# Emptying two kinds of PSUM accumulators on ScalarE or on VectorE, as a planner chooses

## The chip, the core and the metric

The kernel runs on one core of one Trainium2 chip. The metric is device time in microseconds (us); lower is better. TensorE multiplies matrices into PSUM; ScalarE and VectorE can read PSUM, GpSimd cannot. Each engine takes its instructions in the order in which they stand in its own queue, and engines wait for one another through semaphores. In the views of the profile PE is TensorE, PEld its loading of weights, ACT ScalarE, DVE VectorE, POOL GpSimd, and SP the engine that issues nearly all DMAs; L763 is line 763 of the kernel.

## The reference

For 8 batches and 8 heads (sequence 576, head size 64) the attention keeps only the scores that lie within tau of their row's maximum. Its result goes through a gate made by a causal convolution over the sequence, and through two 512x512 products:

```python
scores = scale * np.matmul(q, k.transpose(0, 1, 3, 2))
thresh = np.max(scores, axis=-1, keepdims=True) - tau
scores = np.where(scores >= thresh, scores, -1000000000.0)
attn = np.exp(scores - np.max(scores, axis=-1, keepdims=True))
attn = attn / (np.sum(attn, axis=-1, keepdims=True) + 1e-09)
x = np.matmul(attn, v)          # then heads side by side: [batch, 576, 512]
...
gate_pre += conv_w[k][None, None, :] * xp[:, k:k + S, :]      # k = 0..4, x shifted
gate = 1.0 / (1.0 + np.exp(-gate_pre))
val = x @ w_val
return (gate * val @ w_out).astype(np.float32)
```

Here `scale` is 1/8, tau is 0.02, and all arrays are float32.

## The kernel before, in words

**The work.** A *job* is one batch and one pair of heads (32 jobs); a batch is four jobs. A job has nine *tiles* of scores, each 128 queries by 576 keys: eight for one head, and one that takes the last 64 queries of both heads. Products of full precision are made from parts: a high part (`kh`, `xh`, `gh`) in a fast format and the rest (`kl`, `xl`, `gl`).

The steps of a tile, with their lines:

- TensorE computes the scores into a PSUM room `s` (L556): four matmuls of 288 columns, six for the tile of both heads.
- VectorE takes the negative row maximum, `nm` (L562).
- ScalarE computes `e`, the exponentials (L568), and the threshold from `nm` (L570).
- VectorE keeps the values over the threshold and sums them, `pp` (L589). Only after this is the room `s` free again. There are two such rooms, `s_90` and `s_91`, used in turn for nearly all of the run.
- GpSimd adds a small number to the sums (L609), VectorE takes reciprocals (L611), and GpSimd or ScalarE multiplies (L622, L618).
- TensorE transposes `pp` into a room `tp` (L678, in threes; two rooms), and ScalarE copies that to SBUF as `T` (L689).

When the tiles of half a job are done, TensorE multiplies `T` by the values `v` into an accumulator `acc` (L752). In batches 1 to 7 ScalarE copies this to `xT` (L763), in two pieces per job, of 320 and of 256 columns. In batch 0 VectorE does it, with a multiplication. From `xT` come the parts `xh` (ScalarE, L837) and `xl` (GpSimd, L321), and the convolution: its first tap on GpSimd (L847), four taps on VectorE (L854), in batch 0 on TensorE (L807), then the gate on ScalarE (L862).

After a batch's four jobs come its *products*: `x` by `w_val` into `acc`, gated by VectorE into `g` (L952), split into `gh` and `gl`, and `g` by `w_out` into `acc`. Here `wvh` and `woh` are the high parts of the weights, `wvl` and `wol` the rest; twelve matmuls (L924) make one accumulator of 320 or of 256 columns. ScalarE halves the outputs into `o` (L995), and SP sends them to memory. There are two accumulators, `acc_318` and `acc_319`. They serve the attended values and both products alike, and each is free again when it has been emptied.

**What sets the order.** No loop does. Every operation is first recorded as an `Op` with an engine, a due time, an estimated cost, an estimated time until others may use its result, what it comes after, and the rooms that it takes and gives back. Then `carry_out` (L153) plays the program through: again and again it looks for the operation that can begin earliest by the estimates, the one with the smaller due time among equals, and emits it there and then. The emitted order is fixed; on the chip each engine follows it and waits where its semaphores say. An operation may have several ways, each with its engine and cost; it then stands in the list of every such engine, and whichever can begin it earliest gets it. Before the change only the multiplications by reciprocals have two ways (GpSimd, ScalarE). TensorE gets what can begin, so products fill the time in which the next scores or transposes cannot. A table, `SHIFT`, moves due times by function, engine and phase of the run.

Of the kernel before, what the change touches and what calls it, by code (L numbers as in the profile page):

```python
# [16 lines left out]
ALU = mybir.AluOpType  # L17
# [9 lines left out]
LATE = 1  # L27
# [22 lines left out]
def tile_thresholded_attention_gated_mix(  # L50
# [14 lines left out]
    nc = tc.nc  # L65
# [127 lines left out]
    r_acc = Rooms(None, 0, None, None, None)  # L193
# [23 lines left out]
    r_xT = Rooms(mix, 2, [P, PAD + S], F32, "xT")  # L217
# [487 lines left out]
    class Half:  # L705
# [35 lines left out]
        def attended(self, k):  # L741
            t, j = self.t, self.j
            w, x0 = W[j], PAD + HALVES[j].start

            def attend():
                acc = self.acc = r_acc.take()
                T = self.T[:, :, 0:w]
                for c in (NKC, *range(NKC)):
                    for h, hs in enumerate(HEADS):
                        c0 = (2 * c + h) * D  # L750
                        chunk = 2 * NKC if c == NKC else h * NKC + c
                        nc.tensor.matmul(  # L752
                            acc[hs, :w], t.v[:, c0 : c0 + D], T[:, chunk, :],
                            start=c == NKC, stop=c == NKC - 1, skip_group_check=True,
                        )

            def evacuate():
                if j == 0:
                    t.xT = r_xT.take()
                if t.b < LATE:  # L760
                    nc.vector.tensor_mul(t.xT[:, x0 : x0 + w], self.acc[:, :w], self.R[:, W[0] - w :])
                else:
                    nc.scalar.copy(t.xT[:, x0 : x0 + w], self.acc[:, :w])  # L763

            cost = 5 * w / 600 + 0.1
            gives = [(r_T, lambda: self.T)]
            if j == 1:
                gives.append((r_v, lambda: t.v))
            made = op("PE", k - (1, 1.5)[j], cost, cost + 0.2, attend, [t.got_v, *self.copies], [r_acc], gives)
            cost = 0.31 if j == 0 else 0.255  # L770
            after = [made] if j == 0 else [made, t.got_x]
            gives = [(r_acc, lambda: self.acc)]
            if t.b < LATE:
                cost += 0.085
                after.append(self.inverses(k))
                gives.append((r_R, lambda: self.R))
            t.got_x = op("DVE" if t.b < LATE else "ACT", k - (3, 3.5)[j], cost, cost + 0.2, evacuate, after,
                         [r_xT] if j == 0 else [], gives)
            t.got_half.append(t.got_x)


# [124 lines left out]
    def products(batch, k, last):  # L906
        b = batch.b
        gs, g, o = {}, {}, {}
        taken = {}
# [77 lines left out]
        for f in range(NE):  # L987
            for j in range(2):
                def evacuate(m, f=f, j=j):
                    hs = HALVES[j]  # L990

                    def run():
                        if j == 0:
                            o[f] = r_o.take()
                        nc.scalar.mul(o[f][:, hs], taken["wo", f, j][:, 0 : hs.stop - hs.start], 0.5)  # L995

                    cost = 0.32 if j == 0 else 0.265
                    return op("ACT", k - 5, cost, cost + 0.2, run,
                              [m] + ([outs[f]] if j else []), [r_o] if j == 0 else [],
                              [(r_acc, lambda: taken["wo", f, j])])  # L1000

                outs[f] = product("wo", f, j, lambda c, i: gs[c][i], parts_of, evacuate)
                firsts.setdefault(f, outs[f])
# [117 lines left out]
```

## Time and profile before

| | |
|---|---|
| median of three runs | 733.68 us (733.28 to 734.31) |
| the profiled execution | 734.48 us, of which the program's span 732.6 us |
| TensorE busy | 721.2 us (98%), granted clock 1.0 throughout |
| ScalarE, VectorE, GpSimd busy | 621.4, 600.3 and 530.1 us |
| copies L763 and L995 | 56 and 64, all on ScalarE |

How to read it: "busy" is the union of an engine's instructions. A row of a view with `xcount` is a group of instructions; two numbers behind the bar are busy us and mean ns of one, and behind the next bar the idle time just before them with what ended it. "who <- by" in the view of waits names the engine that sat idle and the instruction that ended the wait. In a timeline, a row has the start, the length, the engine, the line and the operation.

### The profile page before, as it was taken

The numbers are of one execution on the slowest core, as the hardware profiler recorded it, in microseconds if no ns is written. First come the engines' busy times: TensorE is split into PE (matmuls) and PEld (weight loads), VectorE is DVE, ScalarE is ACT, GpSimd is POOL, SyncE is SP. The second block draws the span as 40 slices with busy tenths as digits, with TensorE's granted clock in tenths as the row PEclk, the third lists the DMA queues.
The fourth block names the chain that finished last, engine by engine and source line by source line (L and its number), as shares of the span: only waits on it lengthen the run. The fifth ranks groups of instructions, "written<-read, shape, count | busy, mean of one in ns | idle before, by whom it ended". The sixth has DMA issues, their size and how long they took to land.

```text
span 732.6 us, 16311 instructions
## 1 busy us (share of the span) xinstructions
PE 721.2 (98%) x5454; PEld 613.9 (84%) x5454; DVE 600.3 (82%) x1291; ACT 621.4 (85%) x1448; POOL 530.1 (72%) x886
## 2 busy tenths in 40 slices
PE   8989999999999999999999999999999999999998
PEld 4767778888898888888888888888888988888898
DVE  6899979999888888788888888888888888888730
ACT  6698889999899988888989889898989988888832
POOL 4876568778889757697778786897658887766331
PEclk9999999999999999999999999999999999999999
DMA  7755665636564655346655546555635465540001
GB/s 211 186 154 149 161 156 138 153 97 154 156 176 125 155 134 138 108 125 181 152 138 140 129 120 162 142 129 137 172 101 144 122 159 152 127 112 21 33 34 65
DMA packets 51588, 97.97 MB, mean 134 GB/s; under 512 B 9008, under 2 KB 9520, under 8 KB 51504
## 3 DMA queue, kind: packets, MB, share of 16 engines
q1 hardware_dynamic: 51264, 96.61, 51.1%
q8 instruction: 44, 0.72, 0.5%
q10 hardware_dynamic: 240, 0.31, 0.2%
q14 instruction: 40, 0.33, 0.1%
HBM read 34.62 MB, written 9.44 MB: 60 GB/s over the span
## 4 chain that ended last, share of the span: by engine, by line
PE 89%; ACT 4%; DVE 3%; DMA 2%; POOL 1%; issue 1%; SPq 0%; ACTq 0%; POOLq 0%
PE acc L924 26%; PE s L556 22%; PE acc L752 21%; PE tp L678 18%; ACT e L568 1%; PE acc L807 1%; DVE pp L589 1%; DVE nm L562 1%; DMA q_r<-qT 1%; ACT T L689 1%; DMA pre<-kT 0%; ACT pp L618 0%; ACT nm L570 0%; ACT xh L837 0%; DMA Q<-ql 0%
## 5 line engine op out<-in xcount | busy, mean ns | idle before, releaser
L562 DVE TENSOR_REDUCE nm<-s 128x1 f32<-128x576 f32 x288 | 214.1, 754 | 44.6 <-PE s L556 41.5
L589 DVE SCALAR_TENSOR_TENSOR pp<-s,nm,e 128x576 f32<-128x576 f32 x256 | 207.2, 813 | 33.2 <-ACT nm L570 29.2
L568 ACT ACTIVATE e<-s,nm 128x576 f32<-128x576 f32 x288 | 215.5, 748 | 19.8 <-DVE nm L562 14.8
L689 ACT COPY T<-tp 128x384 f32<-128x384 f32 x384 | 176.2, 487 | 26.2 <-PE tp L678 24.7
L678 PE MATMUL tp<-ident,pp 128*128 128x128 f32 x1152 | 175.3, 273 | 1.1 <-ACT T L689 1.1
L752 PE MATMUL acc<-T,v 128*64 128x256 f32 (+1 forms) x1280 | 169.3, 411 | 0.0
L622 POOL TENSOR_SCALAR pp<-pp,sums 128x576 f32<-128x576 f32 x165 | 137.6, 840 | 39.4 <-DVE sums L611 33.0
L556 PE MATMUL s<-KH,Q 128*128 128x288 f32 x496 | 152.2, 323 | 3.3 <-DVE pp L589 3.1
L678 PEld LDWEIGHTS tp<-ident,pp 128*128 128x128 f32 x1152 | 138.7, 140 | 7.2 <-ACT T L689 1.8
L556 PE MATMUL s<-KL,Q 128*128 128x288 f32 x496 | 138.2, 295 | 0.0
L752 PEld LDWEIGHTS acc<-T,v 128*64 128x64 f32 x1280 | 86.2, 136 | 61.5 <-issue 8.9
L556 PEld LDWEIGHTS s<-KH,Q 128*128 128x128 f32 x496 | 93.4, 188 | 29.0 <-issue 13.7
L854 DVE SCALAR_TENSOR_TENSOR pre<-xT,cw,pre 128x576 f32<-128x576 f32 x112 | 103.3, 922 | 9.1 <-POOL pre L847 8.9
L556 PEld LDWEIGHTS s<-KL,Q 128*128 128x128 f32 x496 | 93.6, 189 | 0.3
L570 ACT ACTIVATE nm<-nm,less 128x1 f32<-128x1 f32 x288 | 85.3, 296 | 0.0
L924 PE MATMUL acc<-gh,woh 128*128 128x320 f32 (+1 forms) x256 | 79.0, 309 | 0.0
L924 PE MATMUL acc<-xl,wvh 128*128 128x320 f32 (+1 forms) x256 | 78.5, 307 | 0.0
L924 PE MATMUL acc<-xh,wvl 128*128 128x320 f32 (+1 forms) x256 | 78.3, 306 | 0.0
L924 PE MATMUL acc<-xh,wvh 128*128 128x320 f32 (+1 forms) x256 | 78.0, 305 | 0.0
L924 PE MATMUL acc<-gl,woh 128*128 128x320 f32 (+1 forms) x256 | 77.9, 304 | 0.0
L924 PE MATMUL acc<-gh,wol 128*128 128x320 f32 (+1 forms) x256 | 77.5, 303 | 0.0
L609 POOL TENSOR_SCALAR sums<-sums 128x2 f32<-128x2 f32 (+1 forms) x144 | 39.7, 276 | 43.0 <-DVE pp L589 30.5
(99 smaller groups left out, 1241.8 us busy)
## 6 DMA issues: line engine op xcount, KB each, us to landing
KH<-kh SPq DMA_DIRECT2D x124, 144.0 KB, 2.6
KL<-kl SPq DMA_DIRECT2D x124, 144.0 KB, 2.9
v<-vs SPq DMA_DIRECT2D x32, 320.0 KB, 3.2
k_r<-kT SPq DMA_DIRECT2D x31, 320.0 KB, 3.8
q_r<-qT SPq DMA_DIRECT2D x31, 288.0 KB, 4.0
outT<-o SPq DMA_DIRECT2D x31, 288.0 KB, 2.1
Q<-qh SPq DMA_DIRECT2D x62, 128.0 KB, 2.3
Q<-ql SPq DMA_DIRECT2D x62, 128.0 KB, 2.4
```

What stands on the lines that cost most here:

```text
L556: nc.tensor.matmul(s[:, a, :HS], w, m, start=i == 0, stop=i == len(terms) - 1)
L562: nc.vector.tensor_reduce(self.nm[:, 0:1], self.s[:, :, :HS], axis=AX.XY, op=ALU.max, negate=True)
L568: nc.scalar.activation(self.e, self.s[:, :, :HS], AF.Exp, bias=self.nm[:, 0:1])
L570: nc.scalar.activation(self.nm[:, 1:2], self.nm[:, 0:1], AF.Identity, bias=less, scale=-1.0)
L589: nc.vector.scalar_tensor_tensor(grp.p[:, i * S : (i + 1) * S].rearrange("p (a f) -> p a f", a=2), self.s[:, :, :HS], self.nm[:, 1:2], self.e,
L609: add = op("POOL", k - 4, 0.2, 0.33, lambda: nc.gpsimd.tensor_scalar(sums(), sums(), 1.0, 1e-9, op0=ALU.mult, op1=ALU.add), [self.kept])
L622: nc.gpsimd.tensor_scalar(v, v, ri(i), 0.0, op0=ALU.mult, op1=ALU.add)
L678: nc.tensor.transpose(tp[:, i * P : (i + 1) * P], self.p[:, k0 : k0 + P], ident)
L689: nc.scalar.copy(T[:, c0 : c0 + n, self.off : self.off + P], tp[:, 0 : n * P].rearrange("p (c q) -> p c q", q=P),)
L752: nc.tensor.matmul(acc[hs, :w], t.v[:, c0 : c0 + D], T[:, chunk, :], start=c == NKC, stop=c == NKC - 1, skip_group_check=True,)
L854: nc.vector.scalar_tensor_tensor(cv, t.xT[:, i : i + S], cw[:, g, i : i + 1], cv, op0=ALU.mult, op1=ALU.add)
L924: nc.tensor.matmul(taken[name, e, j][:, :w], wt[:, c, c0 : c0 + P], moving(c, i)[:, hs], start=n == 0, stop=n == NM - 1,)
```

## The change

Two copies get a second way, on VectorE: that of the attended values in batches 1 to 7 (L763, as a `tensor_copy`) and that of the outputs (L995, as a `tensor_scalar` by 0.5). The planner counts 0.03 us more of VectorE's time for the copy than of ScalarE's, and takes its result as usable 0.03 us sooner.

```diff
-            def evacuate():
+            def evacuate(copy=nc.scalar.copy):
...
                 else:
-                    nc.scalar.copy(t.xT[:, x0 : x0 + w], self.acc[:, :w])
+                    copy(t.xT[:, x0 : x0 + w], self.acc[:, :w])
...
             t.got_x = op("DVE" if t.b < LATE else "ACT", k - (3, 3.5)[j], cost, cost + 0.2, evacuate, after,
-                         [r_xT] if j == 0 else [], gives)
+                         [r_xT] if j == 0 else [], gives,
+                         () if t.b < LATE else
+                         [("DVE", cost + 0.03, cost + 0.17, lambda: evacuate(nc.vector.tensor_copy))])
...
-                    def run():
+                    def run(on="ACT"):
                         if j == 0:
                             o[f] = r_o.take()
-                        nc.scalar.mul(o[f][:, hs], taken["wo", f, j][:, 0 : hs.stop - hs.start], 0.5)
+                        dst, src = o[f][:, hs], taken["wo", f, j][:, 0 : hs.stop - hs.start]
+                        if on == "ACT":
+                            nc.scalar.mul(dst, src, 0.5)
+                        else:
+                            nc.vector.tensor_scalar(dst, src, 0.5, None, op0=ALU.mult)
...
                               [m] + ([outs[f]] if j else []), [r_o] if j == 0 else [],
-                              [(r_acc, lambda: taken["wo", f, j])])
+                              [(r_acc, lambda: taken["wo", f, j])],
+                              [("DVE", cost + 0.03, cost + 0.17, lambda: run("DVE"))])
```

In the order that results, 63 of the 120 copies stand on VectorE: of `xT` 16 of 28 pieces of 320 columns and 11 of 28 of 256, of `o` 21 of 32 and 15 of 32. ScalarE keeps 57. Seven multiplications by reciprocals move from GpSimd to ScalarE as well (L618 stands there 71 times, 64 before). Every other operation stays on its engine, and TensorE has the same 4756 matmuls, but from the first moved copy on, all engines have them in another order. Lines behind the changed functions have higher numbers in the new kernel: L924 became L926, and L995 became L999 on ScalarE and L1001 on VectorE.

The first place is where the orders part. On VectorE before, at the end of batch 1's first half job, the preparation of the weights and the tiles' steps follow one another:

```order
L589 SCALAR_TENSOR_TENSOR pp2_122,sums0_124<-s1_91,nm3_119,e1_115 128x576
L265 TENSOR_SCALAR spare_m_178<-spare1_177 128x256
L267 SCALAR_TENSOR_TENSOR woh_88<-o1_175,spare_m_178 128x256
L562 TENSOR_REDUCE nm0_116<-s0_90 128x1
L562 TENSOR_REDUCE nm1_117<-s1_91 128x1
```

On VectorE after, the same place:

```order
L589 SCALAR_TENSOR_TENSOR pp2_122,sums0_124<-s1_91,nm3_119,e1_115 128x576
L265 TENSOR_SCALAR spare_m_178<-spare1_177 128x256
L763 COPY xT0_136<-acc1_319 128x320
L267 SCALAR_TENSOR_TENSOR woh_88<-o1_175,spare_m_178 128x256
L562 TENSOR_REDUCE nm0_116<-s0_90 128x1
L611 RECIPROCAL sums0_124<-sums0_124 128x2
L562 TENSOR_REDUCE nm1_117<-s1_91 128x1
```

The copy of the attended values has come in ahead of two row maxima; on ScalarE it is gone from between L969 and L369.

The second place is on TensorE, behind the attended values of batch 1's last half job. Before, from the last matmul into the score room `s1_91` on:

```order
L556 MATMUL s1_91<-KL1_111,Q1_107 128x288
L678 MATMUL tp0_92<-ident_85,pp2_122 128x128 x3
L556 MATMUL s0_90<-KH1_109,Q1_107 128x288
L556 MATMUL s0_90<-KL1_111,Q1_107 128x288
L556 MATMUL s0_90<-KH1_109,Q1_107 128x288
L556 MATMUL s0_90<-KL1_111,Q1_107 128x288
L924 MATMUL acc0_318<-gl3_173,woh_88 128x320
L678 MATMUL tp1_93<-ident_85,pp2_122 128x128 x3
L924 MATMUL acc0_318<-gh3_169,wol_89 128x320
L678 MATMUL tp0_92<-ident_85,pp2_122 128x128 x3
L924 MATMUL acc1_319<-gh0_166,woh_88 128x256
L924 MATMUL acc1_319<-gl0_170,woh_88 128x256
```

Nine more such products of 256 columns follow before the next scores into `s1_91`. After, from the same matmul to the next scores into the same room:

```order
L556 MATMUL s1_91<-KL1_111,Q1_107 128x288
L678 MATMUL tp0_92<-ident_85,pp2_122 128x128 x3
L556 MATMUL s0_90<-KH1_109,Q1_107 128x288
L556 MATMUL s0_90<-KL1_111,Q1_107 128x288
L556 MATMUL s0_90<-KH1_109,Q1_107 128x288
L556 MATMUL s0_90<-KL1_111,Q1_107 128x288
L678 MATMUL tp1_93<-ident_85,pp2_122 128x128 x3
L678 MATMUL tp0_92<-ident_85,pp2_122 128x128 x3
L926 MATMUL acc1_319<-xh1_139,wvh_86 128x320
L556 MATMUL s1_91<-KH1_109,Q1_107 128x288
L556 MATMUL s1_91<-KL1_111,Q1_107 128x288
```

The outputs of batch 0, which fill this place before, stand further ahead in the new order and are used up; one product is left here between the two uses of the room.

The third place is the end of the program. The last eight outputs, which stand on ScalarE before, are on VectorE after; its last rows, with `o` the outputs on their way to memory:

```order
L1001 TENSOR_SCALAR o0_174<-acc1_319 128x320
L1001 TENSOR_SCALAR o0_174<-acc0_318 128x256
L1001 TENSOR_SCALAR o1_175<-acc1_319 128x320
L1001 TENSOR_SCALAR o1_175<-acc0_318 128x256
L1001 TENSOR_SCALAR o0_174<-acc1_319 128x320
L1001 TENSOR_SCALAR o0_174<-acc0_318 128x256
```

Nothing else stands behind them on VectorE, and nothing behind the casts of `g` on ScalarE.

## Rows read from the trace of the kernel before

**Rows 1.** The head of the profile's page: the span, the busy time of each engine (share of the span, instructions), and the shares of the chain that ended last.

```profile
span 732.6 us, 16311 instructions
PE 721.2 (98%) x5454; PEld 613.9 (84%) x5454; DVE 600.3 (82%) x1291; ACT 621.4 (85%) x1448; POOL 530.1 (72%) x886
...
PE 89%; ACT 4%; DVE 3%; DMA 2%; POOL 1%; issue 1%; SPq 0%; ACTq 0%; POOLq 0%
```

**Rows 2.** Busy time by stretch: the stretch, its length, then busy us of each engine with its count of instructions, the granted clock, and the share and rate of the DMA engines.

```profile
0.00:117.00 117.00, 110.49 (x714) 83.47 (x716) 99.48 (x239) 95.73 (x233) 77.20 (x159) 1.00 0.64 167
117.00:200.00 83.00, 82.81 (x640) 70.01 (x637) 74.99 (x165) 75.61 (x179) 68.80 (x107) 1.00 0.55 142
200.00:300.00 100.00, 99.94 (x782) 87.06 (x781) 82.89 (x175) 89.05 (x204) 77.16 (x132) 1.00 0.58 146
300.00:400.00 100.00, 98.80 (x770) 85.59 (x769) 86.49 (x184) 90.11 (x209) 80.75 (x127) 1.00 0.54 136
400.00:500.00 100.00, 100.00 (x783) 87.04 (x783) 84.78 (x179) 88.05 (x205) 78.59 (x129) 1.00 0.53 136
500.00:600.00 100.00, 99.88 (x780) 85.95 (x777) 85.28 (x179) 89.74 (x208) 77.73 (x130) 1.00 0.56 142
600.00:702.00 102.00, 102.00 (x797) 87.73 (x796) 78.30 (x164) 84.97 (x198) 61.47 (x98) 1.00 0.34 91
```

**Rows 3.** The view of waits for TensorE, from 117 us to the end: who waited for whom, us in total, times, longest us.

```profile
PE s L556 <- DVE pp L589: 1.2, 1, 1.2
PE tp L678 <- ACT T L689: 0.2, 1, 0.2
```

**Rows 4.** The longest wait of Rows 3 in the timeline from 296 us on, all engines, with rows left out.

```profile
297.20 0.08 DVE L589 DVE_READ_ACCUMULATOR pp<-s,nm,e 128x1 f32 x1
...
298.80 0.74 POOL L377 TENSOR_SCALAR q_r<-q_r,sc 128x576 f32<-128x576 f32 x1 [2.01 <-DMA q_r<-qT]
...
299.62 0.19 POOL L609 TENSOR_SCALAR sums<-sums 128x2 f32<-128x2 f32 x1
299.84 0.17 DVE L611 RECIPROCAL sums<-sums 128x2 f32<-128x2 f32 x1 [2.56 <-POOL sums L609]
299.93 1.40 DVE L562 TENSOR_REDUCE nm<-s 128x1 f32<-128x576 f32 x2
300.05 0.78 ACT L618 ACTIVATE pp<-pp,sums 128x576 f32<-128x576 f32 x1 [2.27 <-DVE sums L611]
...
300.85 0.37 ACT L763 COPY xT<-acc 128x256 f32<-128x256 f32 x1
301.25 0.67 ACT L837 CAST xh<-xT 128x576 fp32r<-128x576 f32 x1
301.83 0.73 ACT L568 ACTIVATE e<-s,nm 128x576 f32<-128x576 f32 x1
...
302.78 0.82 DVE L589 SCALAR_TENSOR_TENSOR pp<-s,nm,e 128x576 f32<-128x576 f32 x1 [1.46 <-ACT nm L570]
```

**Rows 5.** Groups of instructions by line and shape: the copies that can move, the nearest shapes on VectorE, and the multiplication that seven times changes its engine.

```profile
L995 ACT ACTIVATE o<-acc 128x320 f32<-128x320 f32 x32 | 14.1, 441 | 5.3 <-PE acc L924 5.1
L995 ACT ACTIVATE o<-acc 128x256 f32<-128x256 f32 x32 | 12.6, 393 | 5.1 <-PE acc L924 5.0
L763 ACT COPY xT<-acc 128x320 f32<-128x320 f32 x28 | 11.9, 426 | 7.1 <-PE acc L752 6.9
L763 ACT COPY xT<-acc 128x256 f32<-128x256 f32 x28 | 10.4, 371 | 10.8 <-PE acc L752 10.7
L618 ACT ACTIVATE pp<-pp,sums 128x576 f32<-128x576 f32 x59 | 46.2, 784 | 4.7 <-DVE sums L611 4.6
L952 DVE SCALAR_TENSOR_TENSOR g<-pre,acc 128x320 f32<-128x320 f32 x32 | 15.5, 484 | 6.5 <-PE acc L924 6.2
L952 DVE SCALAR_TENSOR_TENSOR g<-pre,acc 128x256 f32<-128x256 f32 x32 | 13.3, 415 | 3.1 <-PE acc L924 2.9
L466 DVE TENSOR_SCALAR pre<-pre,sc 64x320 f32<-64x320 f32 x1 | 0.4, 386 | 0.6 <-DMA pre<-qT 0.6
L466 DVE TENSOR_SCALAR pre<-pre,sc 64x256 f32<-64x256 f32 x1 | 0.4, 353 | 2.2 <-DMA pre<-qT 2.2
```

**Rows 6.** The timeline from 184 to 193 us, the second place of the change in the kernel before: one way of a score room from its matmuls to `pp`. The first two rows and the one at 189.67 give the pace of products of 320 columns (0.15 us from one start to the next) and of transposes.

```profile
184.75 0.31 PE L924 MATMUL acc<-gh,woh 128*128 128x320 f32 x1
184.90 0.81 PE L678 MATMUL tp<-ident,pp 128*128 128x128 f32 x6
...
189.28 0.29 PE L556 MATMUL s<-KL,Q 128*128 128x288 f32 x1
189.41 0.29 PE L556 MATMUL s<-KH,Q 128*128 128x288 f32 x1
189.54 0.29 PE L556 MATMUL s<-KL,Q 128*128 128x288 f32 x1
189.67 0.49 PE L678 MATMUL tp<-ident,pp 128*128 128x128 f32 x3
189.87 0.76 DVE L562 TENSOR_REDUCE nm<-s 128x1 f32<-128x576 f32 x1 [0.61 <-PE s L556]
190.66 0.74 ACT L568 ACTIVATE e<-s,nm 128x576 f32<-128x576 f32 x1
191.30 0.28 ACT L570 ACTIVATE nm<-nm,less 128x1 f32<-128x1 f32 x1
191.62 0.82 DVE L589 SCALAR_TENSOR_TENSOR pp<-s,nm,e 128x576 f32<-128x576 f32 x1
```

**Rows 7.** The waits of ScalarE for the accumulators' matmuls, whole run: us in total, times, longest us.

```profile
ACT xT L763 <- PE acc L752: 17.6, 31, 2.7
...
ACT o L995 <- PE acc L924: 10.1, 10, 1.4
```

**Rows 8.** The end of the timeline: TensorE's last recorded product, and the last copy before the last transfer.

```profile
729.02 0.28 PE L924 MATMUL acc<-gh,wol 128*128 128x256 f32 x1
729.39 0.38 ACT L995 ACTIVATE o<-acc 128x256 f32<-128x256 f32 x1 [0.98 <-PE acc L924]
```

## The prediction

> **What bounds the kernel now.** I read the head of the page first: TensorE is busy 98% of the span, and 89% of the chain that ended last is its own [rows 1]. So the share of ScalarE or VectorE says little; what counts is how long TensorE stands still, and where. The table by stretches answers that [rows 2]. Up to 117 us TensorE is idle for 117.00 - 110.49 = 6.51 us, the beginning of the program among it. From 117 to 702 us the idle times are 0.19, 0.06, 1.20, 0, 0.12 and 0 us, together 1.57 us in 585. The granted clock is 1.00 in every stretch, so it takes no part.
>
> The first moved copy stands at 118 us of the trace, and up to there the two orders agree. Hence the change works only on the stretch with 1.57 us of idle time, and on the end. The view of waits names what this is: one wait of 1.2 us for a `pp` of VectorE and one of 0.2 us for a copy `T` of ScalarE [rows 3]; the rest is too small for a row of its own. TensorE's work itself is the same 4756 matmuls.
>
> The wait of 1.2 us is worth following [rows 4]. GpSimd waited 2.01 us for the DMA of `q_r`; the sums behind it came late; VectorE's next instruction, a reciprocal, needed them, and VectorE did nothing for 2.56 us although two row maxima stood right behind it. The exponentials then queued on ScalarE behind a multiplication (0.78 us), a copy of attended values (0.37 us) and a cast (0.67 us). One of the copies in question is thus on this path, with about 0.4 us, but a late DMA began it.
>
> **The change, part by part.** *ScalarE's load.* It gives up 16 x 0.426 + 11 x 0.371 for `xT` and 21 x 0.441 + 15 x 0.393 for `o` [rows 5], which is 6.8 + 4.1 + 9.3 + 5.9 = 26.1 us, and gets seven multiplications of 0.784 us, 5.5 us. From 621.4 us busy it comes to about 601 us. None of this is on the chain by itself.
>
> *VectorE's load.* No row shows VectorE copying one PSUM operand of 128 partitions. The nearest from above is L952, which reads PSUM and a second operand: 484 and 415 ns. From below it is L466, one operand from SBUF on 64 partitions: 386 and 353 ns [rows 5]. The 37 wide and 26 narrow copies cost 23.5 to 28.7 us; I take 27, nearer to the row that reads PSUM. VectorE goes from 600.3 to about 627 us, the place that ScalarE had. On average the change only exchanges which of the two is the fuller engine; over 585 us, 27 us of copies are 5 points of VectorE's share, and between 117 and 200 us it already stands at 74.99 of 83 us, 90% [rows 2]. What covers these loads is TensorE's own work between two uses of a score room, and this must be checked room by room.
>
> *The score rooms.* One way of a room can be read from its last matmul on [rows 6]: the matmul starts at 189.54 and takes 0.13 us at the pace of its neighbours, so TensorE is through at 189.67; the maximum runs at 189.87, the exponentials at 190.66, the threshold at 191.30, and `pp` from 191.62 to 192.44. That is 2.77 us, and some 0.06 us until TensorE may begin again: 2.83 us. TensorE must have this much other work between two uses of a room, or it waits. I priced TensorE's rows in both orders by their pace: 0.13 us for a matmul of scores, 0.11 for a transpose, 0.145 and 0.115 for products of 320 and 256 columns [rows 6], and so on. Over the some 250 reuses behind the program's beginning the two orders look alike: the middle one is 3.8 us in both, and below 3.2 us lie 23 before and 22 after. But the shortest differ. Before, the shortest behind 118 us has 2.95 us. After, two are too short, both at the second place of the order. The scores in `s1_91` that end the rows shown come after nine transposes (0.98 us), four matmuls of scores (0.53) and one product (0.145): 1.65 us of work for a way of 2.83 us, a wait of 1.2 us. The reuse ahead of it, of `s0_90`, has ten transposes, four matmuls of scores and seven products, 2.62 us: a wait of 0.2 us. A third reuse, with 1.97 us, comes behind the first of these waits and is covered by it. The reason is in the rows: outputs of batch 0 filled this place, and the new order has spent them earlier. So the new order holds **1.4 us** of waiting that the old one does not. No later work gives it back, since TensorE has no idle time left to shorten.
>
> *What goes.* At most the 1.57 us. The wait for `T` is ScalarE's and may go with its load; the wait that a DMA began lies in an order that is now another, and may fall where it hurts or where it does not. I count half, **-0.8 us**.
>
> *Copies that hold VectorE.* A copy that stands in the queue before its matmuls are done stops what is behind it. On ScalarE this happened 41 times, 27.7 us in all, a mean of 0.68 us [rows 7]; it moves with the copies. Behind 33 of the 63 copies the next VectorE instruction is a row maximum or a `pp`, the two steps of a score room's way. I count **+0.5 us**: one such hold of the 0.68 us reaching TensorE in part. The bounds are 0 (reuses have 1 us to spare in the middle) and the rival below.
>
> *The accumulators.* Emptying on VectorE must not take longer than the other accumulator's use. The shortest distance from the end of one use to the next of the same accumulator is 0.72 us of TensorE's work in either order, so nothing is added as long as the copy starts at once.
>
> *The end.* The last copy, 0.38 us after the last product [rows 8], is done by VectorE in 0.35 to 0.42: -0.03 to +0.04 us. Taken as nothing. The DMA queue has the same number of issues; which of them is early decides small things of the kind already counted.
>
> The sum: 1.4 - 0.8 + 0.5 = +1.1 us on the profiled execution of 734.48 us (span 732.6, 1.88 outside it). The median shown, 733.68, is 0.80 us below that execution, so the prediction for a median is 733.68 + 1.1 = about **734.7 us**, +0.14%. A difference under 0.2% (1.47 us) can hardly be told from no change.
>
> **The rivals.** *Nothing is lost, and the waits go.* For it: ScalarE is relieved by 20 us, the long wait of rows 4 has a copy on its path, and the planner chose VectorE only where it expected it to be free. Against it: two places in the new order are too short by the rows. If the 1.57 us go, with some 0.3 us of slowed starts around them, and the 1.4 us do not appear because TensorE comes late to this place for another reason, the time is 733.68 - 1.9 = 731.8 us. That is the most that can be gained.
>
> *VectorE is held by copies ahead of the scores' steps.* Its place is the queue of VectorE, 33 copies with a maximum or a `pp` right behind. If a hold is 0.68 us and the copy itself 0.43, `pp` is 1.1 us late; a reuse with less than 3.2 + 0.7 us, about half of all, then makes TensorE wait for a part. For 33 copies, a third of them held, half of these at a short reuse and 0.7 us each, that is 33 / 3 / 2 x 0.7 = 3.9 us. With the 1.4 us and -0.8: +4.5, or 738.2 us. It decides as soon as more than two such holds reach TensorE in full. For it: the 2.56 us for which a reciprocal held VectorE, which did reach TensorE [rows 4]. Against it: ScalarE was held for 27.7 us and TensorE lost only 0.2 us to its copies behind 117 us [rows 3]. The Trainium skill, "PSUM — Partial Sum Buffer", section "Engine vs sequencer instructions", says that the queues of ScalarE, VectorE and GpSimd are strictly first in, first out. The trace agrees in the 2.56 us just named; by that rule alone a copy placed too early is never passed by.
>
> *The copies stay in effect where they were.* If VectorE's copies happened only where it would be idle anyway and the order's other differences even out, the time is 733.7 us. The order shows 63 copies moved, so this is the case of no effect, not of no change; it lies within the forecast's band.
>
> **How the numbers follow.** The forecast and the case of no effect, within 0.2%, that is 732.2 to 735.15 us: 0.52. Waits gone: 0.09. VectorE held, or the two short places costing more than counted: 0.39. So faster by more than 0.2% 0.09, within 0.52, slower 0.39. The lower end of the range leaves out most of the first rival: 733.68 - 0.9 = 732.8 us. The upper end is just short of the second rival's price, 738.0 us. The likeliest case's own range is 733.2 to 735.2 us.
>
> **What would show it right or wrong.** In the profile of the changed kernel TensorE's waits should hold one of about 1.2 us for a `pp`, near 190 us, with the scores behind one product of `xh` and `wvh`; if TensorE is busy throughout there, that step is wrong. The view of waits for VectorE should show rows of L763 and L1001 that wait for `acc`, a few tenths of a us each; their sum tells whether the holds moved, and TensorE's waits for `pp` tell whether they matter. VectorE should be busy about 627 us and ScalarE about 601. Idle time of TensorE between 117 and 702 us should be 2.5 to 3 us. More than 5 us would mean the second rival, under 1 us the first. A granted clock below 1.00 in any stretch would make the whole sum void.

## The result, and the profile after

| | before | after |
|---|---|---|
| median | 733.48 us (733.05 to 734.31, 4 runs) | 738.62 us (737.55 to 739.83, 4 runs) |
| ratio | | 1.0068 (95% interval 1.0054 to 1.0081) |
| the profiled execution | 734.48 us, span 732.6 | 739.83 us, span 738.0 |

The change costs 5.1 us, 0.7%. It lies outside the range that was given, by 0.6 us.

The head of the page after, in the columns of [rows 1]:

```profile
span 738.0 us, 16350 instructions
PE 726.1 (98%) x5454; PEld 615.5 (83%) x5454; DVE 622.8 (84%) x1354; ACT 606.1 (82%) x1392; POOL 524.1 (71%) x879
```

ScalarE and VectorE have changed places, as the diff says. The profile counts 5454 matmuls in both kernels (not the 4756 named ahead), and TensorE is "busy" with them 4.9 us longer; keep this number, it comes back below. By stretches behind 117 us, in the columns of [rows 2]; in the two left out, 117 to 150 and 400 to 500 us, TensorE is busy throughout:

```profile
150.00:200.00 50.00, 48.51 (x367) 40.89 (x366) 43.24 (x91) 42.66 (x102) 39.63 (x66) 1.00 0.54 143
200.00:300.00 100.00, 99.03 (x764) 85.06 (x763) 88.94 (x188) 85.43 (x193) 75.64 (x127) 1.00 0.56 141
300.00:400.00 100.00, 99.97 (x776) 85.15 (x775) 88.06 (x191) 89.27 (x203) 78.58 (x129) 1.00 0.54 138
...
500.00:600.00 100.00, 99.82 (x775) 86.32 (x773) 87.11 (x184) 87.11 (x197) 74.15 (x120) 1.00 0.55 141
600.00:702.00 102.00, 101.84 (x791) 87.43 (x790) 85.74 (x184) 86.05 (x199) 66.87 (x108) 1.00 0.35 91
```

TensorE's idle time from 117 to 702 us is 0 + 1.49 + 0.97 + 0.03 + 0 + 0.18 + 0.16 = 2.83 us, against 1.57 before. The view of waits for TensorE from 117 us on, beside [rows 3], has three waits for a `pp` where there was one:

```profile
PE s L556 <- DVE pp L589: 2.1, 3, 1.3
PE tp L678 <- ACT T L689: 0.2, 1, 0.2
```

The longest lies at the second place of the change, the one of [rows 6]; here is the timeline, with rows left out:

```profile
187.76 0.29 PE L556 MATMUL s<-KL,Q 128*128 128x288 f32 x1
...
189.96 0.31 PE L926 MATMUL acc<-xh,wvl 128*128 128x320 f32 x1
190.28 0.66 PE L678 MATMUL tp<-ident,pl 128*128 128x128 f32 x4
190.78 0.40 PE L556 MATMUL s<-KH,Q 128*128 128x288 f32 x1
...
194.62 0.30 PE L556 MATMUL s<-KL,Q 128*128 128x288 f32 x1
...
195.61 0.82 PE L678 MATMUL tp<-ident,pp 128*128 128x128 f32 x6
...
196.38 0.41 PE L926 MATMUL acc<-xh,wvh 128*128 128x320 f32 x1
...
198.07 0.40 PE L556 MATMUL s<-KH,Q 128*128 128x288 f32 x1 [1.27 <-DVE pp L589]
```

One product stands between the transposes and the next scores, and TensorE waits for `pp`: 1.27 us in the view, 1.54 us if the starts are compared (198.07 - 196.38, less the 0.15 us that a product takes at its neighbours' pace). The difference is what a modelled end swallows: the product's row is drawn 0.41 us long. The rows ahead show a loss that the view leaves out altogether: at 190.28 the transposes begin 0.32 us after a product that should have taken 0.15, and no idle time is noted.

The second longest wait isn't at a place that the prediction named. It is this one, with rows left out; the first row is the last matmul into the room that the last row takes again:

```profile
281.84 0.30 PE L556 MATMUL s<-KL,Q 128*128 128x288 f32 x1
...
283.51 1.38 DVE L856 SCALAR_TENSOR_TENSOR pre<-xT,cw,pre 128x576 f32<-128x576 f32 x1
...
285.68 0.40 PE L556 MATMUL s<-KH,Q 128*128 128x288 f32 x1 [0.61 <-DVE pp L589]
```

Between the two uses TensorE has four matmuls of scores, six transposes and twelve products, 2.9 us at the prediction's prices and so a little more than the way of 2.83 us that it took for every room. Here the way is 285.68 - 281.84 - 0.13 = 3.71 us: a tap of the convolution (L854 before, L856 here) stands ahead of `pp` on VectorE and takes 1.38 us, where the shortest tap takes 0.79.

The copies that moved, by shape, in the columns of [rows 5], and VectorE's waits for their matmuls from 117 us on, in those of [rows 7]:

```profile
L1001 DVE TENSOR_SCALAR o<-acc 128x320 f32<-128x320 f32 x21 | 10.3, 488 | 7.5 <-PE acc L926 7.5
L763 DVE COPY xT<-acc 128x320 f32<-128x320 f32 x16 | 7.8, 490 | 6.7 <-PE acc L752 6.2
L1001 DVE TENSOR_SCALAR o<-acc 128x256 f32<-128x256 f32 x15 | 6.3, 421 | 5.8 <-PE acc L926 5.7
L763 DVE COPY xT<-acc 128x256 f32<-128x256 f32 x11 | 4.7, 425 | 6.3 <-PE acc L752 6.2
```

```profile
DVE o L1001 <- PE acc L926: 13.2, 17, 1.9
DVE xT L763 <- PE acc L752: 12.4, 17, 2.8
```

On VectorE a copy takes 488 to 490 and 421 to 425 ns, 29.1 us in all; on ScalarE the wide ones took 441 and 426, the narrow ones 393 and 371 [rows 5]. In 34 of 63 cases VectorE stands before the copy and waits for its matmuls, 25.6 us in all.

**A dip of the clock in this one execution.** From 10 to 15 us the granted clock was this, in after:

```profile
10.00:15.00 5.00, 5.00 (x18) 3.64 (x18) 3.80 (x8) 3.60 (x9) 3.70 (x6) 0.66 0.84 231
```

and this before:

```profile
10.00:15.00 5.00, 5.00 (x25) 3.41 (x25) 4.69 (x10) 4.72 (x12) 4.19 (x9) 1.00 0.81 212
```

The first attended values start at 23.73 us instead of 22.07, in the same order of instructions: 1.66 us of the profiled span are this dip. The prediction would have called its sum void at a clock below 1.00, but the dip isn't the result: the other three runs of after have a mean clock of 1.000 and take 737.55 to 739.01 us.

### The profile page after: what moved, and what is told of

Its sections match the earlier page's. It is cut to its first block, busy times and chain, and to the rows that moved or that the text cites. A ratio compares the mean times of both kernels' runs of the same rounds, so it can differ in the third digit from the quotient of the medians.

```text
span 738.0 us, 16350 instructions
## 1 busy us (share of the span) xinstructions
PE 726.1 (98%) x5454; PEld 615.5 (83%) x5454; DVE 622.8 (84%) x1354; ACT 606.1 (82%) x1392; POOL 524.1 (71%) x879
## 4 chain that ended last, share of the span: by engine, by line
PE 84%; DVE 6%; ACT 5%; POOL 2%; issue 1%; DMA 1%; SPq 0%; POOLq 0%; ACTq 0%
PE acc L926 23%; PE s L556 21%; PE acc L752 21%; PE tp L678 17%; DVE pp L589 2%; DVE nm L562 2%; ACT e L568 1%; DVE pre L856 1%; PE acc L809 1%; ACT T L689 1%; DMA pre<-qT 1%; ACT nm L570 1%; ACT pp L618 0%; DMA Q<-ql 0%; ACT xh L839 0%
## 5 line engine op out<-in xcount | busy, mean ns | idle before, releaser
L689 ACT COPY T<-tp 128x384 f32<-128x384 f32 x384 | 174.2, 485 | 33.5 <-PE tp L678 32.2
L622 POOL TENSOR_SCALAR pp<-pp,sums 128x576 f32<-128x576 f32 x160 | 131.7, 829 | 34.7 <-DVE sums L611 29.3
L856 DVE SCALAR_TENSOR_TENSOR pre<-xT,cw,pre 128x576 f32<-128x576 f32 x112 | 102.0, 910 | 0.2
L926 PE MATMUL acc<-gh,woh 128*128 128x320 f32 (+1 forms) x256 | 79.4, 310 | 0.1
L926 PE MATMUL acc<-xl,wvh 128*128 128x320 f32 (+1 forms) x256 | 78.5, 307 | 0.0
L926 PE MATMUL acc<-xh,wvl 128*128 128x320 f32 (+1 forms) x256 | 78.4, 306 | 0.0
L926 PE MATMUL acc<-xh,wvh 128*128 128x320 f32 (+1 forms) x256 | 78.3, 306 | 0.0
L926 PE MATMUL acc<-gl,woh 128*128 128x320 f32 (+1 forms) x256 | 78.2, 306 | 0.0
L926 PE MATMUL acc<-gh,wol 128*128 128x320 f32 (+1 forms) x256 | 77.9, 304 | 0.0
```

Of the source, the lines that this page charges most:

```text
L622: nc.gpsimd.tensor_scalar(v, v, ri(i), 0.0, op0=ALU.mult, op1=ALU.add)
L689: nc.scalar.copy(T[:, c0 : c0 + n, self.off : self.off + P], tp[:, 0 : n * P].rearrange("p (c q) -> p c q", q=P),)
L856: nc.vector.scalar_tensor_tensor(cv, t.xT[:, i : i + S], cw[:, g, i : i + 1], cv, op0=ALU.mult, op1=ALU.add)
L926: nc.tensor.matmul(taken[name, e, j][:, :w], wt[:, c, c0 : c0 + P], moving(c, i)[:, hs], start=n == 0, stop=n == NM - 1,)
```

## The experiments

The theories, in the form that they had at the end; the expectations quoted below were written before each group of runs and word them as they then stood:

- *Engine* (theory B in the expectations): the copies hold VectorE's queue, so row maxima and `pp` come late (the second rival of the prediction). Then the loss hangs on the copies ahead of these steps, and an unchanged order with the copies on VectorE shows it.
- *Order* (theory A): the new order has reuses of a score room that are too short, the second place above all. Then the new order shows it with every copy on ScalarE.
- *Fit* (theory D, and in e3 a part of A): the old order and the old engines together suit the chip unusually well, and nearly any other plan loses some us. Then a plan that differs for a trivial reason loses as much, with no copy on VectorE.

Theory C, slow copies or copies that disturb the other engines, falls in its plain form with e1: its copies take 0.47 to 0.49 us and 0.41 to 0.43 us, and GpSimd is busy no longer there than in e12, the kernel before (529.2 us for 531.7).

All results, the difference against the runs of the kernel before on the same chip (medians 733.07, 733.45 and 733.95 us for the three groups). Some runs have a mean granted clock below 1.000; the last column has the median of the runs whose mean granted clock was 1.000, and their number (the kernel before: 732.8, 733.5 and 733.95 in such runs).

| | median us | ratio and interval | difference us | at clock 1.000 |
|---|---|---|---|---|
| e1 old order, new engines | 738.97 | 1.0077 (1.0065 to 1.0089) | +5.9 | 738.3 (3) |
| e2 new order, old engine | 739.83 | 1.0093 (1.0080 to 1.0106) | +6.8 | 739.9 (3) |
| e3 before, one price + 0.01 | 738.99 | 1.0085 (1.0065 to 1.0104) | +5.9 | 736.7 (3) |
| e4 after, other table | 738.36 | 1.0074 (1.0059 to 1.0089) | +5.3 | 737.9 (1) |
| e5 e1, 33 copies ahead of a score step | 736.44 | 1.0038 (1.0025 to 1.0051) | +3.0 | 736.7 (4) |
| e6 e1, the other 30 copies | 736.10 | 1.0034 (1.0021 to 1.0047) | +2.65 | 736.1 (6) |
| e7 before, another price + 0.01 | 739.08 | 1.0081 (1.0065 to 1.0096) | +5.6 | 739.1 (6) |
| e8 before, other table | 735.14 | 1.0023 (1.0013 to 1.0033) | +1.7 | 734.4 (7) |
| e9 only outputs have two ways | 737.72 | 1.0052 (1.0040 to 1.0064) | +3.8 | 737.6 (3) |
| e10 only attended values have | 737.88 | 1.0057 (1.0042 to 1.0072) | +3.9 | 737.8 (4) |
| e11 after, price + 0.01 | 740.16 | 1.0088 (1.0073 to 1.0103) | +6.2 | 739.4 (2) |
| e12 before again, one run | 732.93 | | | 732.9 (1) |

### Engines without the order, order without the engines

e1 keeps the plan of before and names the engine of each copy by a list, the same 63 copies on VectorE as after:

```diff
+X_ON_DVE = list("10010000101100111001000110101011011110101000100110000111")
...
-                    nc.scalar.copy(t.xT[:, x0 : x0 + w], self.acc[:, :w])
+                    copy = nc.vector.tensor_copy if X_ON_DVE.pop(0) == "1" else nc.scalar.copy
+                    copy(t.xT[:, x0 : x0 + w], self.acc[:, :w])
```

> The kernel before with its order on TensorE, GpSimd and SyncE unchanged row for row; only the same 63 copies as in the change are done by VectorE, each at its own place in the old order. Theory A (the order that the planner makes is what costs: TensorE's work runs out at a few places): within 1.5 us of before, 732 to 735 us. Theory B (copies on VectorE hold the score tiles' steps behind them in its queue): most of the change's loss, 736.5 to 738.5 us. Theory C (VectorE's copies are slow or disturb ScalarE's and GpSimd's accesses): the same as B, with copies of well over 0.48 and 0.42 us.

e2 plans as after, and where the planner took VectorE's way, ScalarE does the copy:

```diff
-                         [("DVE", cost + 0.03, cost + 0.17, lambda: evacuate(nc.vector.tensor_copy))])
+                         [("DVE", cost + 0.03, cost + 0.17, lambda: evacuate())])
...
-                              [("DVE", cost + 0.03, cost + 0.17, lambda: run("DVE"))])
+                              [("DVE", cost + 0.03, cost + 0.17, lambda: run())])
```

> The changed kernel with its order on TensorE, GpSimd and SyncE unchanged row for row, but every copy done by ScalarE, at its place in the new order. Theory A: the loss stays, 737 to 740 us, somewhat more than the change where the copies crowd ScalarE. Theories B and C: the loss goes, 733 to 735 us.

Measured: +5.9 and +6.8 us. Each half of the change costs as much as the whole or more, so they don't add up, and neither theory alone is enough. In the new order VectorE's copies don't cost anything and may help: after is 738.62, the same order on ScalarE alone 739.83, with intervals that just meet.

In e1 the rows of TensorE are those of before, one by one, so one place can be laid beside the same place of before. This is the timeline of e12, the kernel before run once more, with weight loads left out:

```profile
591.63 1.22 DVE L854 SCALAR_TENSOR_TENSOR pre<-xT,cw,pre 128x576 f32<-128x576 f32 x1
...
592.22 0.31 PE L924 MATMUL acc<-gl,woh 128*128 128x320 f32 x1
592.37 0.29 PE L556 MATMUL s<-KH,Q 128*128 128x288 f32 x1
592.44 0.41 ACT L995 ACTIVATE o<-acc 128x256 f32<-128x256 f32 x1
...
592.77 0.80 DVE L589 SCALAR_TENSOR_TENSOR pp<-s,nm,e 128x576 f32<-128x576 f32 x1
...
593.81 0.29 PE L556 MATMUL s<-KH,Q 128*128 128x288 f32 x1
```

and of e1, where L857 is L854, L1000 the copy of the outputs on VectorE, L591 `pp`, L558 the scores and L927 the products:

```profile
596.38 0.31 PE L927 MATMUL acc<-gl,woh 128*128 128x320 f32 x1
596.51 1.23 DVE L857 SCALAR_TENSOR_TENSOR pre<-xT,cw,pre 128x576 f32<-128x576 f32 x1
596.65 0.40 PE L558 MATMUL s<-KH,Q 128*128 128x288 f32 x1
...
597.66 0.41 DVE L1000 TENSOR_SCALAR o<-acc 128x256 f32<-128x256 f32 x1
...
598.00 0.80 DVE L591 SCALAR_TENSOR_TENSOR pp<-s,nm,e 128x576 f32<-128x576 f32 x1
...
598.86 0.40 PE L558 MATMUL s<-KH,Q 128*128 128x288 f32 x1 [0.50 <-DVE pp L591]
```

The copy now stands between a tap of the convolution and a `pp`. Counted from the product, `pp` begins 1.07 us later than before; 0.35 us of this is the copy, and 0.72 us was there already in front of the tap, so VectorE came late to the place. From the product to the second set of scores it takes 593.81 - 592.22 = 1.59 us before and 598.86 - 596.38 = 2.48 us in e1: 0.89 us lost, of which the view names 0.50. The first 0.12 us (596.65 - 596.38 = 0.27 against 0.15) have no idle time in TensorE's row.

How the loss of e1 grows is seen in the starts of two blocks of attended values. The same blocks, first in e12 and then in e1:

```profile
295.63 0.65 PE L752 MATMUL acc<-T,v 128*64 128x256 f32 x4
...
697.75 0.44 PE L752 MATMUL acc<-T,v 128*64 128x256 f32 x2
```

```profile
298.80 0.65 PE L754 MATMUL acc<-T,v 128*64 128x256 f32 x4
...
703.08 0.44 PE L754 MATMUL acc<-T,v 128*64 128x256 f32 x2
```

It is 3.17 us at the first and 5.33 at the second. The view of waits of e1, from 117 us on, names only 1.3 us in all:

```profile
PE s L558 <- DVE pp L591: 0.7, 2, 0.5
PE acc L927 <- DVE o L1000: 0.2, 1, 0.2
PE tp L680 <- ACT T L691: 0.2, 1, 0.2
PE s L558 <- DVE pl L591: 0.2, 1, 0.2
```

TensorE's busy time is 726.8 us in e1 and 722.3 in e12, with the same matmuls in the same order: 4.5 of the 5.3 us of span stand there as "busy".

Since the order is the same, all 5454 starts can be laid against those of e12. From 117 us on e1 falls 5.3 us behind, and 4.5 us of this stand at 14 places that cost 0.15 to 0.76 us each. At eleven places, 3.5 us together, the wait of the matmul or of its weight load ends with a step of VectorE. But that step isn't always late behind a copy. The second most costly place, first in e12 and then in e1, with rows left out:

```profile
133.62 0.42 DVE L260 SCALAR_TENSOR_TENSOR spare<-o,spare_m 128x256 int32<-128x256 int32 x1
...
135.19 0.29 PE L556 MATMUL s<-KH,Q 128*128 128x288 f32 x1
```

```profile
133.87 1.10 DVE L262 SCALAR_TENSOR_TENSOR spare<-o,spare_m 128x256 int32<-128x256 int32 x1
...
135.76 0.40 PE L558 MATMUL s<-KH,Q 128*128 128x288 f32 x1 [0.16 <-DVE pl L591]
```

In the 6 us ahead of it no copy stands on VectorE. A step of the weights' preparation (L260, in e1 L262) took 1.10 us instead of 0.42, and the `pl` behind it came late. GpSimd lies otherwise beside it: its `kl` runs from 133.35 us for 1.33 us in e1, from 133.83 us for 0.94 us in e12. The taps behave alike: in e1 the 112 taps take 0.79 to 1.52 us, 35 of them over 0.9 us, and each of these ran beside a GpSimd step for a third of its time or more; `pp`, which reads PSUM, stays between 0.80 and 0.82 us. Three further places of e1, at 177, 230 and 295 us, lie behind a tap that took 1.39 to 1.52 us, for 0.81 to 1.00 in e12. That GpSimd is what lengthens these steps is argued from the rows; no run varied it alone. All of VectorE's instructions but the copies take only 1.6 us longer in e1 together, so it matters where the long ones fall.

### Which copies cost

e5 and e6 are e1 with shorter lists: the 33 copies behind which a row maximum or a `pp` stands in VectorE's queue, and the other 30.

```diff
-O_ON_DVE = list("1110000111101001100101101000111000100110110000101100111011111111")
+O_ON_DVE = list("1010000011101001100101101000100000100110110000101100000000000000")
```

> The order of before on TensorE, as in e1_engine_only (which lost 5.9 us), but only 33 of the 63 copies are on VectorE: those that stand there right ahead of a row maximum or of the step that keeps a tile's values. Theory B (a copy delays the score tile's step behind it): most of that loss, 736.5 to 739 us. Theory D (the old order fits the chip, and whatever is moved costs, about as the number moved): 33/63 of it, about 736 us.

> As e5_held_only, with the other 30 copies on VectorE: those ahead of a convolution tap, a reciprocal, a step of the weights, or the end. Theory B: little, 733 to 734.5 us. Theory D: 30/63 of the loss of e1_engine_only, about 736 us.

Measured: +3.0 and +2.65 us, together 5.65, nearly e1's 5.9. It is 0.09 us for each copy of either kind, so standing ahead of a score step isn't what makes a copy dear. This is a mean and not a price: by the starts, six places of 0.15 us or more make 1.8 us in e5, and ten make 3.2 us in e6, some of which is given back. Of e1's 14 places 13 are found again in e5 or in e6; the largest, at 598.86 us, is in neither. The same last block as above starts at 699.56 us in e5 and at 700.55 in e6. That is 1.81 and 2.80 us behind e12; the profiled execution of e5 is the fastest of its seven.

### Plans that differ for a trivial reason

In e3 and e7 no copy has a second way. The kernel is that of before, except that the planner believes one copy to take 0.01 us longer: that of the outputs in e3, that of the attended values in e7. e11 does the like to the change.

```diff
-                    cost = 0.32 if j == 0 else 0.265
+                    cost = 0.33 if j == 0 else 0.275
```

```diff
-            cost = 0.31 if j == 0 else 0.255
+            cost = 0.32 if j == 0 else 0.265
```

```diff
-                         [("DVE", cost + 0.03, cost + 0.17, lambda: evacuate(nc.vector.tensor_copy))])
+                         [("DVE", cost + 0.04, cost + 0.18, lambda: evacuate(nc.vector.tensor_copy))])
```

> The kernel before, without any way for VectorE; only the planner's price of the output copies is 0.01 us higher (0.33 and 0.275 instead of 0.32 and 0.265), which makes it choose another order. By the planner's own figures TensorE's idle time behind 100 us is then 3.5 us, against 1.3 before and 4.4 in the change. Theory A (any new order gives up what the old one was fitted for): 1.5 to 3.5 us slower than before, 735 to 737 us. Theories B and C: no copy moves, so no loss, 733 to 734.5 us.

> The kernel before, without any way for VectorE; the planner's price of the copy of attended values is 0.01 us higher (0.32 and 0.265 instead of 0.31 and 0.255), which makes another order, as in e3_nudge with the other copy (5.9 us slower). Theory D: slower again by 3 to 7 us, 736 to 740 us. If e3_nudge was an accident: 733 to 735 us.

> The changed kernel with the planner's price of the VectorE way 0.01 us higher (0.04 more than ScalarE's instead of 0.03), which makes another order, as e3_nudge and e7_nudge_xT do for the kernel before. Theory D: no worse than any new order, 736 to 741 us, with a scatter of a us or two about the change. If the change's order was an unlucky one: 733 to 736 us.

Measured: +5.9, +5.6 and +6.2 us. e3 has three runs at a lower clock; without them it is +4.0, more than either expectation with them and inside that of theory A without. All runs of e7 have a clock of 1.000. In each plan other waits are the long ones. The longest groups of TensorE's waits from 117 us on, two of e3 and then the first of e11:

```profile
PE s L556 <- DVE pp L589: 1.5, 2, 1.3
PE tp L678 <- POOL pp L622: 1.0, 1, 1.0
```

```profile
PE acc L926 <- POOL xl L321: 1.6, 2, 1.1
```

This is the strongest result: 0.01 us in an estimate, with every copy on the engine where it was, costs 4.0 and 5.6 us, about as much as the change. The loss doesn't need copies on VectorE.

### Other tables, and halves of the change

If the table of shifts suits the old plan alone, another table may suit the new one. I let the planner try many tables of two dozen entries and kept that with the least idle time of TensorE by its own count: e4 for the change, e8 for the kernel before.

```diff
-    ("Tile.multiply", "PE"): (0, 0, -8),
+    ("Tile.multiply", "PE"): (-0.5, 0, -4.75),
...
+    ("Tile.weigh", "ACT"): (-8.0, -2.25, 0),
```

> The changed kernel with another table of shifts of due times, found by trying tables until the planner's own idle time of TensorE was small (0.5 us behind 100 us, against 1.3 before and 4.4 in the change). VectorE still takes about half of the copies. Theory A: as fast as before or up to 1.5 us faster, 731.5 to 734 us. Theories B and C: as slow as the change, 736.5 us or more.

> The kernel before, without any way for VectorE, with a table of shifts found in the same way as that of e4_retuned_after (planner's own idle time of TensorE behind 100 us 0.6, against 1.3 before). If the planner's figure decides: 732 to 733 us. Theory D (the planner's figure leaves out what the chip does, and the old order is the one that fits): 736 to 740 us, like e4_retuned_after.

Measured: +5.3 and +1.7 us (+0.9 at clock 1.000). By the planner's own count TensorE idles 0.5 us behind 100 us in e4, 0.6 in e8, 1.3 in the kernel before and 3.5 in e3. This count doesn't foretell the chip: e4 has less than before and takes 5.3 us more. One reason may lie in the kernel: the planner keeps GpSimd and those steps of VectorE that work from SBUF apart in time (L159, L175) and counts a tap as 0.74 us (L876). On the chip 97 of the 112 taps of e1 overlap a GpSimd step, and a tap takes up to 1.52 us. e8, at 735.14 us, meets neither of the two expectations; it shows that a wholly different plan can come within 1 to 2 us.

e9 takes the second way from the attended values, e10 from the outputs:

```diff
-                         () if t.b < LATE else
-                         [("DVE", cost + 0.03, cost + 0.17, lambda: evacuate(nc.vector.tensor_copy))])
+                         ())
```

```diff
-                              [("DVE", cost + 0.03, cost + 0.17, lambda: run("DVE"))])
+                              [])
```

> One half of the change: only the copies of outputs may go to VectorE (36 of 64 do, in yet another order). Theory D (whatever new order, about the same loss): 736 to 740 us. If the change's parts add up: half of its 5 us, 735.5 to 736 us.

> The other half: only the copies of attended values may go to VectorE (27 of 56 do). Theory D: 736 to 740 us. If the change's parts add up: the rest of its 5 us, 735.5 to 736 us.

Measured: +3.8 and +3.9 us, with 36 and 27 copies on VectorE. Neither half is the one that costs.

### The kernel before once more

e12 is the kernel before, unchanged, for a second profile.

> The kernel before, unchanged, for a second trace. If the wait of 1.2 us behind a late DMA at 303 us was an accident of the profiled execution, it is missing here, TensorE's idle time from 117 to 702 us is 0.2 to 0.5 us instead of 1.57, and the time is about 733 us. If it belongs to the kernel, it is here again, and the time is about 734.5 us.

Measured: 732.93 us, and the wait of 1.2 us from which the prediction had taken its gain isn't there. The view of waits for TensorE from 117 us on has one row left of [rows 3]:

```profile
PE tp L678 <- ACT T L689: 0.2, 1, 0.2
```

Its beginning, in the timeline beside [rows 4]:

```profile
297.22 0.75 POOL L377 TENSOR_SCALAR q_r<-q_r,sc 128x576 f32<-128x576 f32 x1 [0.84 <-DMA q_r<-qT]
...
298.27 0.17 DVE L611 RECIPROCAL sums<-sums 128x2 f32<-128x2 f32 x1 [1.39 <-POOL sums L609]
```

and the stretch behind it, in the columns of [rows 2]:

```profile
300.00:400.00 100.00, 99.97 (x778) 86.82 (x777) 86.95 (x186) 89.90 (x210) 80.80 (x129) 1.00 0.55 139
```

The DMA of `q_r` is waited for by 0.84 us instead of 2.01, the reciprocal holds VectorE for 1.39 us instead of 2.56, and TensorE stands still for 0.03 us in this stretch instead of 1.20. Over 117 to 702 us it idles 0.42 us. The wait in [rows 4] was an accident of one execution.

## Why the prediction was wrong

The forecast was +1.1 us, the result +5.1. (733.68 + 1.1 is 734.8 us, not 734.7.) The step that failed is the one on the score rooms: one way of a room, 2.83 us, was taken for all, and every reuse with more work than that was put at nothing. By its steps:

- *The second place, +1.4 us:* right in its place and a little short in size. The wait is where it was put, 1.27 us in the view and 1.54 by the starts, for 1.2. The reuse of `s0_90` ahead of it has 190.78 - 187.76 - 0.13 = 2.89 us from the room's last matmul to the next scores, for 2.62 us of work: 0.27 us late, for 0.2, part of it in front of the transposes of `pl`.
- *What goes, -0.8 us:* wrong. There was nothing to go. The 1.57 us of idle time came from one profiled execution; a second one has 0.42. Half of an accident was counted as a gain.
- *The other reuses of a score room, put at nothing:* this is the step that failed. The orders "look alike" in how much work TensorE has between two uses, but the way of a room isn't 2.83 us everywhere: it is 3.32 us at the second place (198.07 - 194.62 - 0.13) and 3.71 at 285.68 us. Take the start of each matmul against the middle distance that e12 has for the same two kinds of matmul, without those of the attended values among themselves. From 117 us to 29 us before the end, e12 has four starts that are 0.15 us or more late, 1.1 us together; after has sixteen, 5.7 us. The difference of 4.6 us is nearly the whole loss. Some 2.1 us of the 5.7 lie from 190 to 198 us, 0.77 at 285.68, and eleven others take 0.19 to 0.38 each; nine of the sixteen, 4.2 us, wait for a step of VectorE. With every copy on ScalarE (e2) the sum is 5.9 us, 3.6 of it behind VectorE, so the copies aren't what makes these ways long.
- *Copies that hold VectorE, +0.5 us:* not a term of its own. VectorE waits 34 times, 0.75 us on average, where 0.68 was taken, so the holds moved as described. With the old order the same 63 copies cost 5.9 us (e1); in the new order taking them back costs another 1.2 (e2 against after). One number for both can't be right.
- *The sum as idle time.* Take the profiled span of after, 738.0 us, less the dip of 1.66, against 731.2 in e12: 5.1 us. Of these, 2.83 - 0.42 = 2.4 us are idle time that the profile shows, the second place among it. The other 2.7 us stand as busy time of TensorE (from the first attended values to 117 us it idles 3.5 and 3.6 us, behind 702 us 3.3 and 3.4, so they are not there).
- *"Idle time of TensorE between 117 and 702 us should be 2.5 to 3 us. More than 5 us would mean the second rival":* the measure was right, 2.83, and it was the wrong measure. A matmul's row is drawn longer than its pace (0.31 us for 0.15), so a wait of some tenths hides in it. The time can grow by 5 us while the idle time that is shown grows by half of that.
- *ScalarE about 601 us busy and VectorE about 627:* 606.1 and 622.8. A copy on VectorE costs 488 to 490 and 421 to 425 ns, 29.1 us in all, a little over the upper bound of 28.7, where 27 was taken. VectorE's busy time still grows by only 22.5 us, because "busy" is a union: rows that follow one another at once are drawn overlapping (the tap at 596.51 us ends at 597.74, the copy behind it starts at 597.66), and VectorE's other rows add up to 0.8 us less. ScalarE's rows add up to 22.5 us less, its union to 15.3. The Trainium skill, "VectorE: DVE Perf Modes", section "The TRN2 errata", gives 120 cycles and one per element at 0.96 GHz for PSUM to SBUF, by which I estimate 458 and 392 ns; these rows are some 30 ns longer.
- *The accumulators:* nearly nothing, as counted. e1 has a single wait of 0.2 us for a copy of outputs.
- *The end:* nothing, as counted. The last copy of after takes 0.42 us, for 0.38 in [rows 8].

*The rivals.* "VectorE is held" had 738.2 us, close to the time. That was luck. A late VectorE is real: at eleven places of e1 TensorE waits for it. But copies right ahead of the scores' steps aren't the cause of the number: e6, whose copies don't stand there, loses as much per copy, e3 and e7 lose about as much with no copy on VectorE, and in the new order VectorE's copies cost nothing (e2). "The waits go" falls with e12.

What holds against all runs is the theory of fit. Under the old plan TensorE idles 0.42 us in 585; every other plan or choice of engines tried costs 1.7 to 6.8 us (e8, the least, 0.9 at clock 1.000), whether it differs by engines, by order or by 0.01 us in an estimate. The late starts go with it: 1.1 us in e12, 2.5 in e8, 4.5 to 5.9 in after and the seven other new orders. The change is one of these plans, about as bad as a nudge. Fit is a description and not a mechanism; what the rows add is that in six of these eight plans more than half of the late time waits for a step of VectorE.

Open: by what road each of the 63 copies shifts VectorE against GpSimd in e1; the places and the long steps are shown, the road from a copy to a long step isn't. What makes the way long at each of the sixteen late starts of after was followed at 285.68 us alone. Whether some table, chosen by times on the chip instead of the planner's count, brings the change below 733 us wasn't tried. No version here beat the kernel before.

## What to carry to other kernels

Where the bound engine idles 0.4 us in 585, a planner's new freedom can only be judged beside a control: the old plan with one estimate moved by 0.01 us; if that loses as much, the loss is the re-plan and not the idea. Before a wait is counted as a gain, a second profile of the same kernel should show it. A loss on TensorE is read from its starts, block against block, because idle time leaves out what modelled ends cover: here about half of the loss, and in e1 most of it. And one way of a buffer, measured at one quiet place, isn't the way everywhere: here 2.83 us became 3.32 and 3.71.

## What the runs showed of the hardware

The dip of the clock at the start wasn't expected. By single microseconds, the profile of after has a granted clock of 0.54 from 11 to 12 us, 0.50 from 12 to 14 and 0.76 from 14 to 15, then 1.00 again; 0.50 is the lower level, 1.2 GHz. From 8 to 10 us, ahead of it, TensorE had been busy 0.57 of 2 us; in the profile of before, whose clock stayed at 1.00, it was 0.76. It cost 1.66 us, once, which is more than several of the differences under study; only the list of clocks run by run tells it apart.

The second thing is the length of VectorE's steps. Those that read a score room in PSUM keep theirs in e1: `pp` 0.80 to 0.82 us, `nm` 0.73 to 0.76. A tap, which reads and writes SBUF, takes 0.79 to 1.52 us with the same shape. None of the 15 taps of e1 that ran with no GpSimd step beside them took over 0.9 us. No run here shows more than that they go together.
